# A three-stage kernel on one core: feed-forward groups begun one group later in TensorE's order, a third load buffer, accumulators copied by ScalarE

## The chip, the cores and the metric

The kernel runs on one core of a Trainium2 chip. The metric is device time in microseconds (us) of one execution. Engine names: TensorE (PE in the profile; PEld is its weight load), VectorE (DVE), ScalarE (ACT), GpSimd (POOL) and SyncE (SP), which here issues all the DMAs.

## The reference

Three computations follow each other; sizes are batch 4, sequence 768, model width 384.

```
# 1. a recurrence with a 48x48 state for each of 4 x 8 heads
for t in range(768):
    y[:, :, t] = r_t @ (state + (u * k_t) v_t)
    state = w_t * state + k_t v_t
# 2. a feed-forward block of width 1024 with a convolution over time as its gate
h = max(x @ w_in, 0)                       # 384 -> 1024
x = (h * sigmoid(conv3(h, conv_w))) @ w_out   # 1024 -> 384
# 3. four single-head attention experts (width 64, causal); the two with the larger
#    gate logits are added for each token, with softmax weights
```

## The kernel before, in words

The function `phase1` does steps 1 and 2; the class `Attention` does step 3. A few matmuls of step 3 (the projections of its first batch) run at the end of step 2.

**Recurrence.** It is cut into 32 units: 4 batches x 2 halves of the sequence (384 tokens) x 4 pairs of heads. For unit u there are

- `load(u)`: two DMAs, `wkr` (decays, k and r with the head dimension on the partitions; two buffers) and `rkv` (v, and r and k by token; three buffers);
- `prep(u)`: on VectorE two scans over the decays (L208 `Dp`, L211 `Fp`), then K (L214) and Q (L216); on GpSimd two products (L218, L219), and their sum `e` on VectorE (L221). Dp, K and Q have three buffers, Fp has two;
- `check(u)`: on ScalarE two passes over the decays (L229) that write into Fp's buffer and so come after K;
- `trans(u)`: TensorE transposes K (L252), ScalarE copies it to KT (L254);
- `scores(u)`: TensorE (L238), then GpSimd and VectorE put the masked scores into `AT` (L241, L244);
- `state(u)`: TensorE (L264), VectorE brings the states forward (L268, L271);
- `yout(u)`: TensorE (L285, L291), ScalarE and VectorE split the result into a high and a low part `Y` (L297, L298), and two or four DMAs bring Y into `X` of its half-sequence (L306).

**Feed-forward.** Each of the eight half-sequences, once its X is complete (after four units), has eight groups of 128 hidden columns, 64 groups in all. Group g has `mlp1(g)` (nine matmuls from X, L322, into the only PSUM buffer `hs`; ScalarE reads it out to `ht`, L326), `conv(g)` (ScalarE L335, two steps on VectorE, L341 and L342 in one half and L337 and L339 in the other, Tanh on ScalarE L345, the product `gt` on VectorE L347) and, four groups later (`LAG`), `mlp2(g)` (L360), which adds into three accumulators `x0` to `x2` with one PSUM buffer each. After the eighth group of a half-sequence the accumulators are copied to `xs` and stored; copies 0 and 1 are ScalarE's (L368), copy 2 VectorE's (L366). Inside group 0 to 5 also stand the splits of the feed-forward weights (`split_w`), in groups 8 to 15 a check of them (`check_w`).

**Order.** TensorE's order in this phase is the written one (`tc.manual_schedule`). The order of every other engine's queue, SyncE's among them, is chosen by a planner when the program is built, from its own estimate of times; within a queue instructions run in order. The written loop takes iteration u as: `trans(u)`, group 2u - G0, `scores(u)`, `state(u)`, `load(u+3)`, `check(u-1)`, `yout(u-1)`, `prep(u+1)`, group 2u - G0 + 1, with G0 = 10. A group of this order is `mlp1(g)`, `conv(g)` and `mlp2(g-4)`. The last unit whose Y belongs to a half-sequence has its `yout` in iteration 4, 8, 12 and so on; with G0 = 10 the first group of that half-sequence is the first group of the next iteration.

Of the kernel before, what the change touches and what calls it, by code (L numbers as in the profile page):

```python
# [10 lines left out]
F32 = mybir.dt.float32  # L11
# [14 lines left out]
HP = H // 2  # L26
# [5 lines left out]
NWKR = 1 + NW + 2 * HT  # L32
# [6 lines left out]
LAG = 4  # L39
# [2 lines left out]

LO_ON_DVE = (("win", 3),)
DIAG_ON_DVE = (6, 7, 8)
X2_ON_DVE, V_ON_DVE, OUT_ON_DVE = (2,), (1,), (5,)
SCALED_ON_POOL = 13


# [42 lines left out]
def phase1(tc, nc, a, x2, ident, stat, lim, top, right, left2):  # L91
# [3 lines left out]
    ld = s1.enter_context(tc.tile_pool(name="ld", bufs=3, side="left"))  # L95
# [14 lines left out]
    def split(u):  # L110
        return u // (2 * HP), u // HP % 2, u % HP

    def load(u):
        b, h, hp = split(u)
        q = b * HP + hp
        x = ld.tile([128, NWKR], F32, name="wkr", bufs=2)
        nc.sync.dma_start(x, a["wkr"][q, h])
        z = ld.tile([128, NRKV], F32, name="rkv")
        nc.sync.dma_start(z, a["rkv"][q, h])
        w, k, r = x[:, 0:NW + 1], x[:, NW + 1:NW + 1 + HT], x[:, NW + 1 + HT:]  # L120
        k, r = (y.rearrange("p (c t) -> p c t", c=CH) for y in (k, r))
        v = z[:, 0:2 * CH * 64].rearrange("p (c j e) -> p c j e", c=CH, j=2)
        rn, kn = (z[:, o:o + 2 * CH * D].rearrange("p (j c d) -> p j c d", j=2, c=CH)
                  for o in (2 * CH * 64, 2 * CH * (64 + D)))
        T[u] = dict(w=w, k=k, r=r, rn=rn, kn=kn, v=v)
# [77 lines left out]
    def prep(u):  # L203
        b, h, hp = split(u)
        t = T[u]
        Dp = wk.tile([128, CH, C + 1], F32, name="Dp")
        w = t["w"]
        nc.vector.tensor_tensor_scan(fl(Dp), w[:, 0:NW], fl(cD), 0.0, op0=OP.mult, op1=OP.add)  # L208
        nc.vector.reciprocal(cF[:, :, C:C + 1], Dp[:, :, C:C + 1])
        Fp = wk.tile([128, CH, C + 1], F32, name="Fp", bufs=2)  # L210
        nc.vector.tensor_tensor_scan(fl(Fp)[:, ::-1], w[:, 1:NW + 1][:, ::-1], fl(cF)[:, ::-1], 0.0,  # L211
                                     op0=OP.mult, op1=OP.add)
        K = wk.tile([128, CH, C], F32, name="K")
        nc.vector.tensor_tensor(K, t["k"], Fp[:, :, 1:C + 1], op=OP.mult)  # L214
        Q = wk.tile([128, CH, C], F32, name="Q")
        nc.vector.tensor_tensor(Q, t["r"], Dp[:, :, 0:C], op=OP.mult)  # L216
        m = t["rn"]
        (nc.vector if u in DIAG_ON_DVE else nc.gpsimd).tensor_tensor(m, m, t["kn"], op=OP.mult)  # L218
        nc.gpsimd.tensor_tensor(m, m, u_b[:, hp][:, :, None].to_broadcast([128, 2, CH, D]), op=OP.mult)  # L219
        e = wk.tile([128, 2, CH], F32, name="e")  # L220
        nc.vector.tensor_reduce(e, m, axis=AX.X, op=OP.add)  # L221
        t.update(Dp=Dp, Fp=Fp, K=K, Q=Q, e=e)

    def check(u):
        t = T[u]
        w, Fp = t["w"], t["Fp"]
        wc = w[:, 1:].rearrange("p (c t) -> p c t", c=CH)[:, :, 0:C]
        for z in range(2):
            nc.scalar.activation(Fp[:, :, 0:C], wc, AF.Relu, bias=lim[:, z:z + 1], scale=(-1.0, 1.0)[z],  # L229
                                 accum_out=stat[:, 2 * u + z:2 * u + z + 1])  # L230

    def scores(u):
        t = T[u]
        sc = [ps_s.tile([128, CH, C], F32, name="sc") for j in range(2)]
        for c in range(CH):
            for j in range(2):
                p = slice(64 * j, 64 * j + 64)
                nc.tensor.matmul(sc[j][:, c], t["K"][p, c], t["Q"][p, c], start=True, stop=True)  # L238
        AT = t["AT"] = wk.tile([128, 2, CH, C], F32, name="AT")
        for j in range(2):  # L240
            nc.gpsimd.affine_select(AT[:, j], t["e"][:, j][:, :, None].to_broadcast([128, CH, C]),  # L241
                                    pattern=[[0, CH], [1, C]], compare_op=OP.is_equal, fill=0.0, base=0,
                                    channel_multiplier=-1)
            nc.vector.copy_predicated(AT[:, j], msk, sc[j])  # L244

    def trans(u):
        b, h, hp = split(u)
        t = T[u]
        n = CH - h
        kt = ps_m.tile([128, CH, 128], F32, name="m")  # L250
        for c in range(n):
            nc.tensor.transpose(kt[:, c], t["K"][:, c], ident)  # L252
        KT = t["KT"] = wk.tile([128, CH, 128], F32, name="KT")
        nc.scalar.activation(KT[:, 0:n], kt[:, 0:n], AF.Copy)  # L254

    def state(u):
        b, h, hp = split(u)
        t = T[u]
        n = CH - h
        U = ps_m.tile([128, CH, D], F32, name="m")  # L260
        for c in range(n):
            for j in range(2):
                p = slice(64 * j, 64 * j + 64)
                nc.tensor.matmul(U[p, c], t["KT"][:, c, p], t["v"][:, c, j, 0:D], start=True, stop=True)  # L264
        Sb = Ss[hp]
        P = t["Dp"][:, :, C:C + 1]
        o = CH * h
        nc.vector.tensor_tensor(Sb[:, o:o + n, 0:D], U[:, 0:n], P[:, 0:n].to_broadcast([128, n, D]), op=OP.mult)  # L268
        for c in range(n):
            if o + c:  # L270
                nc.vector.scalar_tensor_tensor(Sb[:, o + c, 0:D], Sb[:, o + c - 1, 0:D], P[:, c], Sb[:, o + c, 0:D],  # L271
                                               op0=OP.mult, op1=OP.add)
# [3 lines left out]
    def yout(u):  # L276
        b, h, hp = split(u)
        t = T[u]
        y = ps_m.tile([128, CH, C], F32, name="m")
        Sb = Ss[hp]  # L280

        for cc in range(CH):
            for j in range(2):
                p = slice(64 * j, 64 * j + 64)
                nc.tensor.matmul(y[p, cc], t["v"][:, cc, j], t["AT"][:, j, cc], start=(cc == 0), stop=False,  # L285
                                 skip_group_check=True)
        for cc in range(CH):
            c = CH * h + cc
            for j in range(2 if c else 0):
                p = slice(64 * j, 64 * j + 64)  # L290
                nc.tensor.matmul(y[p, cc], Sb[p, c - 1], t["Q"][p, cc], start=False, stop=(cc == CH - 1),  # L291
                                 skip_group_check=True)
        Y = wk.tile([128, 2, HT + 4], F32R, name="Y", bufs=2)[:, :, 0:HT + 4 * h]
        if h:
            nc.scalar.activation(Y[:, :, 0:4], _f(YP.pop(hp)), AF.Copy)
        yf = y.rearrange("p c t -> p (c t)")
        nc.scalar.activation(Y[:, 0, 4 * h:], yf, AF.Copy)  # L297
        nc.vector.tensor_tensor(Y[:, 1, 4 * h:], yf, _f(Y[:, 0, 4 * h:]), op=OP.subtract)  # L298
        if not h:
            YP[hp] = wk.tile([128, 2, 4], F32R, name="YP", bufs=HP)  # L300
            nc.scalar.activation(YP[hp], _f(Y[:, :, HT - 4:]), AF.Copy)
        bh = 2 * b + h
        if bh not in X:
            X[bh] = xp.tile([128, 3, 2, HT + 4 * h], F32R, name=f"X{h}")
        for s, n, i, d in _moves(hp):
            nc.sync.dma_start(_f(X[bh][d:d + n, i]), _f(Y[s:s + n]))  # L306
        del T[u]
# [63 lines left out]


    NG = B * 2 * NF
    G0 = 2 * (HP + 1)

    def group(g):
        if 0 <= g < NG:
            mlp1(g)
            conv(g)
        if 0 <= g < 6:  # L380
            split_w(("win", "wout")[g % 2], (win, wout)[g % 2], g // 2 + 1)
        if NF <= g < 2 * NF:
            check_w(("win", "wout")[g % 2], (g - NF) // 2)
        if g == 2 * NF:
            rawc.close()
        if 0 <= g - LAG < NG:
            mlp2(g - LAG)

    with tc.manual_schedule(engines={mybir.EngineType.PE}):
        prep(0)  # L390
        for u in range((NG + LAG + G0 + 1) // 2):
            if u < 2 * NU:
                trans(u)
            group(2 * u - G0)
            if u < 2 * NU:
                scores(u)
                state(u)
                if u + 3 < 2 * NU:
                    load(u + 3)
            if 0 < u <= 2 * NU:  # L400
                check(u - 1)
                yout(u - 1)
            if u + 1 < 2 * NU:
                prep(u + 1)
            if u == 1:
                conv_w()
                split_w("win", win, 0)
            if u == 2:
                split_w("wout", wout, 0)
            if u == 2 * NU:  # L410
                s1.close()
                left2()
            group(2 * u - G0 + 1)

# [631 lines left out]
```

## Time and profile before

| | |
|---|---|
| median of 3 runs | 700.2 us (697.96 to 701.39) |
| the profiled execution's own time | 698.2 us |
| its span, first to last instruction | 696.4 us |
| mean granted TensorE clock | 0.945 of full speed |
| busy: TensorE / its weight loads | 590.6 / 467.8 us |
| busy: VectorE, ScalarE, GpSimd | 510.8, 348.0, 189.3 us |

The profile is one execution, read out by the hardware profiler; its rows are given below, where the prediction needs them. An engine's busy time leaves out its waits; a wait is put down to what ended it. Shares over the whole span mix the two phases, so they are read stage by stage. The granted clock is what the throttle let TensorE have: 1.00 is 2.4 GHz, 0.50 is 1.2 GHz, and a value between them means that a stretch had both.

### The profile page before, as it was taken

The page shows a single profiled execution, that of the slowest core. Times are in us where ns is not written, and L with a number is a line of the kernel's source. Part 1 is how long each engine was busy: PE and PEld are TensorE (multiplying, and loading weights), DVE is VectorE, ACT ScalarE, POOL GpSimd, SP SyncE. Part 2 cuts the span into 40 slices and gives each one's busy share as a digit, 9 for nine tenths or more (in the row PEclk, how much of TensorE's full clock was granted, in tenths as well). Part 3 has the DMA queues.
Part 4 walks back from the last instruction along what each step waited for, and adds up shares of the span by engine and source line. Part 5 has one row for each costly group of instructions (what it writes and reads, how often), then busy time and mean ns, then how long its engine had stood idle before and what let it go on. Part 6 is the DMA issues. An engine that isn't in the chain of part 4 may idle for free. (4 is left out here: it accounts for less than half of the span.)

```text
span 696.4 us, 11267 instructions
## 1 busy us (share of the span) xinstructions
PE 590.6 (85%) x3978; PEld 467.8 (67%) x3978; DVE 510.8 (73%) x1163; ACT 348.0 (50%) x843; POOL 189.3 (27%) x209
## 2 busy tenths in 40 slices
PE   3352588897997997989989999998999899899996
PEld 3231466675765775666767677696898788789664
DVE  7999569788786987787986565378875777587471
ACT  3252684444454453544443445265555655556462
POOL 7677123223142321332231062002002100300360
PEclk9975679899999999999989999999999999999999
DMA  8487674444352553443431255236415432551502
GB/s 308 157 306 226 229 245 118 121 143 130 105 170 80 153 149 94 151 141 99 148 92 46 69 167 164 61 102 171 102 54 152 128 91 66 147 137 59 147 2 72
DMA packets 34400, 92.38 MB, mean 133 GB/s; under 512 B 5024, under 2 KB 14368, under 8 KB 34336
## 3 DMA queue, kind: packets, MB, share of 16 engines
q1 hardware_dynamic: 34336, 91.59, 44.6%
q8 instruction: 33, 0.54, 0.3%
q14 instruction: 31, 0.25, 0.1%
HBM read 53.77 MB, written 9.44 MB: 91 GB/s over the span
## 5 line engine op out<-in xcount | busy, mean ns | idle before, releaser
L322 PE MATMUL hs<-X,win 128*128 128x384 f32 (+1 forms) x576 | 127.4, 368 | 46.4 <-DMA X<-Y 15.1
L322 PEld LDWEIGHTS hs<-X,win 128*128 128x128 f32 x576 | 105.0, 200 | 56.7 <-issue 16.3
L360 PE MATMUL x<-gt,wout 128*128 128x386 f32 (+1 forms) x384 | 140.0, 502 | 2.4 <-DVE xs L366 2.4
L360 PEld LDWEIGHTS x<-gt,wout 128*128 128x128 f32 x384 | 75.1, 198 | 41.7 <-DVE xs L366 5.3
L782 ACT ACTIVATE A<-sm,mn 128x128 f32<-128x128 f32 (+5 forms) x96 | 63.7, 665 | 26.3 <-DVE mn L781 25.7
L229 ACT ACTIVATE Fp<-wkr,lim 128x384 f32<-128x384 f32 x64 | 39.1, 611 | 69.1 <-DVE K L214 61.9
L218 POOL TENSOR_TENSOR rkv<-rkv 128x288 f32<-128x288 f32 x29 | 30.6, 1054 | 147.8 <-DMA rkv<-in_rkv 141.8
L781 DVE CUSTOM_DVE_ANT_0 sm<-st,mask 128x128 f32<-128x128 f32 (+5 forms) x96 | 58.0, 618 | 16.6 <-PE st L768 16.1
L345 ACT ACTIVATE st<-ct 128x382 f32<-128x382 f32 (+1 forms) x64 | 33.4, 521 | 54.6 <-DVE ct L342 29.2
L241 POOL TENSOR_SCALAR_AFFINE_SELECT AT<-e 128x384 f32<-128x384 f32 x64 | 44.6, 719 | 49.9 <-DVE e L221 49.9
L347 DVE SCALAR_TENSOR_TENSOR gt<-st,ht 128x382 f32<-128x382 f32 (+1 forms) x64 | 37.5, 587 | 24.0 <-ACT st L345 22.8
L802 PE MATMUL t<-ident,A 128*128 128x128 f32 x336 | 53.5, 275 | 1.7 <-ACT T L806 0.9
L768 PE MATMUL st<-sk,sq 128*128 128x384 f32 (+3 forms) x128 | 44.4, 358 | 3.1 <-DVE mn L781 2.2
L680 POOL TENSOR_TENSOR xs<-x,xs 128x768 fp32r<-128x768 f32 x12 | 22.4, 1882 | 87.5 <-ACT xs L679 87.5
L244 DVE COPY_PREDICATED AT<-msk,sc 128x384 f32<-128x384 uint32 x64 | 36.1, 585 | 13.5 <-PE sc L238 13.5
L808 DVE COPY T<-t 128x128 f32<-128x128 f32 (+3 forms) x64 | 32.2, 504 | 18.6 <-PE t L802 18.1
L802 PEld LDWEIGHTS t<-ident,A 128*128 128x128 f32 x336 | 40.4, 140 | 7.5 <-POOL A L795 1.9
L768 PE MATMUL st<-sl,sq 128*128 128x384 f32 (+3 forms) x128 | 40.9, 333 | 4.9 <-DMA sl<-kl 4.8
L326 ACT ACTIVATE ht<-hs 128x384 f32<-128x384 f32 (+1 forms) x64 | 30.8, 482 | 27.1 <-PE hs L322 26.9
L818 PE MATMUL m<-T,V 128*64 128x384 f32 (+2 forms) x288 | 43.3, 421 | 0.0
L219 POOL TENSOR_TENSOR rkv<-rkv,u_b 128x288 f32<-128x288 f32 x32 | 35.2, 1100 | 29.5 <-DVE rkv L218 25.0
L341 DVE SCALAR_TENSOR_TENSOR ct<-ht,cwk,ct 128x386 f32<-128x386 f32 x32 | 25.1, 785 | 23.0 <-ACT ct L335 23.0
(129 smaller groups left out, 1167.9 us busy)
## 6 DMA issues: line engine op xcount, KB each, us to landing
wkr<-in_wkr SPq DMA_DIRECT2D x32, 578.0 KB, 4.6
rkv<-in_rkv SPq DMA_DIRECT2D x32, 480.0 KB, 3.5
rawt<-in_win SPq DMA_DIRECT2D x8, 768.0 KB, 5.1
rawt<-in_wout SPq DMA_DIRECT2D x8, 768.0 KB, 5.1
sk<-kh SPq DMA_DIRECT2D x32, 192.0 KB, 3.3
sl<-kl SPq DMA_DIRECT2D x32, 192.0 KB, 4.1
x<-x SPq DMA_DIRECT2D x12, 384.0 KB, 4.2
out_dram<-ot SPq DMA_DIRECT2D x24, 192.0 KB, 2.0
```

The lines of the kernel that those rows point to most:

```text
L219: nc.gpsimd.tensor_tensor(m, m, u_b[:, hp][:, :, None].to_broadcast([128, 2, CH, D]), op=OP.mult)
L229: nc.scalar.activation(Fp[:, :, 0:C], wc, AF.Relu, bias=lim[:, z:z + 1], scale=(-1.0, 1.0)[z], accum_out=stat[:, 2 * u + z:2 * u + z + 1])
L241: nc.gpsimd.affine_select(AT[:, j], t["e"][:, j][:, :, None].to_broadcast([128, CH, C]), pattern=[[0, CH], [1, C]], compare_op=OP.is_equal ...
L244: nc.vector.copy_predicated(AT[:, j], msk, sc[j])
L322: nc.tensor.matmul(hs[:, 0:N], win[wi][:, f // 2, i, (f % 2) * 128:(f % 2 + 1) * 128], x[:, i, xi], start=(n == 0), stop=(n == 8))
L347: nc.vector.scalar_tensor_tensor(gt, st, 1.0, ht[:, o:o + N], op0=OP.add, op1=OP.mult)
L360: nc.tensor.matmul(acc[0][i][:, 0:N], wout[:, f, i * 128:(i + 1) * 128], gt, start=(f == 0), stop=(f == NF - 1))
L768: nc.tensor.matmul(st[:, z, 0:n], q[:, qi * C:(qi + 1) * C], k[:, z * n:(z + 1) * n], start=(i == 0), stop=(i == 1))
L781: nc.vector.tensor_tensor_reduce(o3, i3, m3, 1.0, 3e38, op0=OP.add, op1=OP.min, accum_out=mn)
L782: nc.scalar.activation(at, o3, AF.Exp, bias=mn, scale=-1.0, accum_out=rs[:, qi % 3:qi % 3 + 1])
L802: nc.tensor.transpose(pt[:, ki - k0], at[:, ki * C:(ki + 1) * C], self.ident)
L818: nc.tensor.matmul(po[o, lo:HT], V[:, ki, (2 * p + j) * 64:(2 * p + j + 1) * 64], Ts[j][:, ki, lo:], start=(ki == 0), stop=(ki == n - 1))
```

## The change

Three edits. `G0` becomes 11, so that group 2u - 11 follows `trans(u)` and group 2u - 10 ends the iteration: every group stands one place later in TensorE's order against the recurrence, and the first group of a half-sequence is no longer next to the last of the one before; the loop gets one turn more to hold the last group. `wkr` takes the pool's own three buffers in place of two. The third accumulator's copy goes from VectorE to ScalarE.

```diff
-X2_ON_DVE, V_ON_DVE, OUT_ON_DVE = (2,), (1,), (5,)
+X2_ON_DVE, V_ON_DVE, OUT_ON_DVE = (), (1,), (5,)
...
     def load(u):
-        x = ld.tile([128, NWKR], F32, name="wkr", bufs=2)
+        x = ld.tile([128, NWKR], F32, name="wkr")
...
-    G0 = 2 * (HP + 1)
+    G0 = 2 * (HP + 1) + 1
...
-        for u in range((NG + LAG + G0 + 1) // 2):
+        for u in range((NG + LAG + G0 + 2) // 2):
```

## Rows read from the trace of the kernel before

**Rows 1.** Windows by stage: length, busy PE, PEld, DVE, ACT, POOL, PEclk, DMA, GB/s.

```profile
0.00:70.76 70.76, 24.98 (x213) 18.82 (x213) 65.19 (x97) 25.65 (x59) 51.39 (x58) 0.80 0.76 250
70.76:124.63 53.87, 38.82 (x287) 31.33 (x287) 39.47 (x76) 35.32 (x78) 12.24 (x16) 0.82 0.61 198
124.63:360.93 236.30, 214.64 (x1527) 161.22 (x1527) 191.95 (x361) 108.94 (x267) 69.45 (x80) 0.96 0.43 127
360.93:404.35 43.42, 42.24 (x283) 31.55 (x283) 24.79 (x52) 18.31 (x43) 6.49 (x14) 0.93 0.23 66
404.35:452.24 47.89, 45.67 (x200) 34.60 (x199) 25.03 (x33) 22.41 (x46) 14.71 (x14) 1.00 0.46 128
452.24:696.40 244.16, 224.29 (x1474) 190.29 (x1474) 164.38 (x547) 137.41 (x352) 35.07 (x30) 0.99 0.38 102
```

**Rows 2.** TensorE's timeline, first group and one border: start, us, instructions, idle before.

```profile
70.76 3.25 PE L322 MATMUL hs<-X,win 128*128 128x384 f32 x9 [10.81 <-DMA X<-Y]
...
163.35 1.88 PE L322 MATMUL hs<-X,win 128*128 128x388 f32 x9
...
167.01 0.38 PE L252 MATMUL m<-ident,K 128*128 128x128 f32 x2
...
171.44 2.29 PE L322 MATMUL hs<-X,win 128*128 128x384 f32 x9 [4.05 <-DMA X<-Y]
173.52 3.31 PE L360 MATMUL x<-gt,wout 128*128 128x386 f32 x6
...
179.47 1.83 PE L322 MATMUL hs<-X,win 128*128 128x384 f32 x9
...
183.09 0.38 PE L252 MATMUL m<-ident,K 128*128 128x128 f32 x2
```

**Rows 3.** Six gaps before a half-sequence's first group, by windows: one, and their sum.

```profile
118.71:124.63 5.92, 0.49 (x5) 0.28 (x3) 5.65 (x10) 1.53 (x5) 1.43 (x2) 0.72 0.49 141
...
sum 26.68, PE 2.25 PEld 1.21 DVE 25.40 ACT 9.03 POOL 8.54; mean PE 0.37 PEld 0.20 DVE 4.23 ACT 1.50 POOL 1.42
```

**Rows 4.** The first group behind each of these gaps: one, and the sum of six.

```profile
360.93:367.76 6.83, 6.83 (x17) 4.60 (x17) 4.11 (x9) 3.71 (x10) 1.31 (x2) 0.55 0.11 23
...
sum 34.20, PE 34.00 PEld 23.99 DVE 14.91 ACT 15.95 POOL 6.15; mean PE 5.67 PEld 4.00 DVE 2.48 ACT 2.66 POOL 1.02
```

**Rows 5.** VectorE's waits, 124.63 to 360.93: engine, line, ender, total us, times, longest.

```profile
DVE gt L347 <- ACT st L345: 14.6, 20, 1.3
DVE ct L341 <- ACT ct L335: 12.1, 12, 3.4
DVE ct L337 <- ACT ct L335: 5.8, 8, 1.5
DVE AT L244 <- PE sc L238: 5.5, 5, 1.5
DVE e L221 <- POOL rkv L219: 2.3, 2, 1.6
```

**Rows 6.** VectorE's timeline: a subtraction for Y, two scans, a wait between them.

```profile
167.28 0.54 DVE L298 TENSOR_TENSOR Y<-m,Y 128x384 fp32r<-128x384 f32 x1
...
203.41 0.96 DVE L208 TENSOR_TENSOR_SCAN Dp<-wkr,cD 128x387 f32<-128x387 f32 x1
...
210.25 0.62 DVE L337 SCALAR_TENSOR_TENSOR ct<-ht,cwk,ct 128x381 f32<-128x381 f32 x1 [0.47 <-ACT ct L335]
...
214.35 1.56 DVE L208 TENSOR_TENSOR_SCAN Dp<-wkr,cD 128x387 f32<-128x387 f32 x1
```

**Rows 7.** SyncE's queue at the same border.

```profile
167.85 2.55 SPq L306 DMA_DIRECT2D X<-Y  x4
```

**Rows 8.** ScalarE's timeline: accumulator copies, and a check behind K.

```profile
192.53 0.86 ACT L368 ACTIVATE xs<-x 128x386 f32<-128x386 f32 x2
...
206.95 0.61 ACT L229 ACTIVATE Fp<-wkr,lim 128x384 f32<-128x384 f32 x1 [2.92 <-DVE K L214]
```

**Rows 9.** Groups by line: VectorE's accumulator copies, whole span.

```profile
L366 DVE COPY xs<-x 128x382 f32<-128x382 f32 (+1 forms) x8 | 4.4, 549 | 6.1 <-PE x L360 6.1
```

## The prediction, made before the change was run

> **What bounds the kernel now.** I read the busy shares by stage first, because the kernel is two programs in a row: a first phase with the recurrence and the feed-forward groups, and attention after it. [rows 1] cut the span at the starts of TensorE's feed-forward groups. The reader is to see three things. In the prologue (0 to 70.76 us) VectorE is busy 65.19 us and TensorE 24.98, so VectorE sets the pace. In the long middle, 124.63 to 360.93, TensorE is busy 214.64 of 236.30 us and VectorE 191.95: neither is full. From 452.24 on TensorE is busy 224.29 of 244.16 us, and the diff touches nothing there.
>
> Second, TensorE's timeline at one border between two half-sequences [rows 2]. The last group before the border ends, two transposes follow at 167.01, and the next group's first matmul starts at 171.44 after 4.05 us of idleness that the DMA into X ended. The half-sequence is eight groups, and such a gap comes back with each, every 236.30 / 5 = 47.3 us; [rows 3] hold six of them, 26.68 us in all, in which TensorE worked 2.25 us.
>
> Third, what the other engines did in these gaps: in the same [rows 3] VectorE was busy 25.40 of the 26.68 us. So TensorE waits for X, but X is late because VectorE is behind. In [rows 6] the subtraction that makes the low part of X runs at 167.28, almost 4 us after the matmuls that it reads (they ended as the group at 163.35 began [rows 2]); [rows 7] show SyncE issuing the four pieces from 167.85 for 2.55 us, and then they fly.
>
> Last, the price behind a gap: the first group after the one shown runs from 171.44 to the end of the output matmuls at 176.83 [rows 2], 5.39 us. The same two lines later, at full clock, go from 179.47 to 183.09, 3.62 us. [rows 4] show the worst of the six, 6.83 us at a mean granted clock of 0.55, that is for the most part at 1.2 instead of 2.4 GHz; before each of them TensorE had stood still, as [rows 3] show.
>
> **The change part by part.**
>
> *Groups one slot later.* Before, an iteration was: transposes, even group, scores and state and output of the recurrence, odd group. The even group that opens a half-sequence came right behind the last group of the one before. After, the opener moves to the end of its iteration. Between the output matmuls whose result X needs and X's first use there were one group and the transposes (163.35 to 167.39); now there are a group (3.66), transposes (0.38), a group (3.62) and the scores to outputs (from 176.83 to 179.47, 2.64): 10.3 us. X arrived 8.1 us after 163.35. So the wait for X goes, with 2 us to spare. All that a group issues moves along, its ScalarE and VectorE instructions too; the weight splits and checks traced inside a group were not held to their place before (the queues of the other engines are the planner's), so I move them by nothing.
>
> How much of this reaches the end? TensorE's side of the middle: its five gaps (the sum less the one shown [rows 3]) are 20.76 us with 1.76 us of work in them, 19.0 lost; the five slow first groups behind the borders that lie at or after its start (the sum less the one shown [rows 4]) are 34.20 - 6.83 = 27.37 us against 5 x 3.62 = 18.1, 9.3 lost. Together 28. VectorE's side is less, and VectorE is what was busy in the gaps. Its idle time there by cause is in [rows 5]. The waits for the scores matmuls, 5.5 us, are there because TensorE stood still. The waits for ScalarE's first convolution product are 12.1 + 5.8 = 17.9 us in 20 waits; away from a border one is 0.47 [rows 6], so at least 17.9 - 20 x 0.47 = 8.5 of it is the border's. The wait for rkv, 2.3, follows from a load whose buffer TensorE freed late. That makes 16.3 us that VectorE can win back. The waits for tanh (14.6 us, 20 of them) are the ping-pong of two in-order queues in every iteration and stay. That they are VectorE's own period shows in [rows 6]: the scan recurs at 203.41 and 214.35, 10.94 us apart, with no border between, while TensorE needs the 10.3 summed above. I take VectorE's 16.3, not TensorE's 28, since its row is the nearer one (95% busy in the gaps); 28 stays as the end of the range.
>
> *All accumulators by ScalarE.* Eight VectorE copies of 549 ns go [rows 9], five of them in the middle: 2.7 us off the pacing engine. ScalarE copies two in 0.86 us [rows 8], so a third costs it 0.43, on an engine busy 108.94 of 236.30 us [rows 1]. Behind the copies the next half-sequence's first output matmuls wait, since the accumulators have one buffer. Three in a row end 0.43 us after two, 3.4 us over eight borders if TensorE waited for each; before, the third was VectorE's at 549 ns. I cost it at nothing, under the cover of the matmuls of the group in between; if the copies are caught behind a wait of ScalarE, see the third rival.
>
> So the rows make the third copy no slower on ScalarE than on VectorE [rows 8, 9]. The Trainium skill, "TensorEngine Tiling (Array Packing)", section "PSUM Bottleneck", says to use both ScalarE and VectorE for emptying PSUM; this part of the change does the opposite. By that rule the gain would be the 3.4 us smaller; by the rows it is not, because VectorE is the engine with the queue, and no run so far shows all three on one engine.
>
> *Third load buffer.* No row of [rows 5] is a wait for wkr, so in the middle it buys nothing. In the prologue it lets the third unit's load leave earlier, and VectorE may then take the recurrence before the weight splits. VectorE's idle time there is 70.76 - 65.19 = 5.6 us [rows 1]; TensorE's wait for the first X is 10.81 us [rows 2]. A gain is between 0 and 10.81, a loss up to about 5.6 if the larger first burst delays what VectorE needs. I take 0: VectorE is 92% busy and reordering makes no less work.
>
> *First stage, 70.76 to 124.63.* Now scores, state and outputs (2.6 us at full clock) fit into the 10.81 us wait for the first X, and the gap at 118.71 (5.92 us with 0.49 of work [rows 3], so 5.4) goes. The ends are 0 and 8. VectorE is idle 53.87 - 39.47 = 14.4 us of this stage [rows 1], a larger share than in the middle, so more of it can be won than there. I take 5.
>
> *Last stage, 360.93 to 404.35.* VectorE is busy 24.79 of 43.42, so TensorE paces. The slow first group, 6.83 against 3.62 us, is won back: 3.
>
> *End of the first phase.* One more group now comes after the recurrence. TensorE is 45.67 of 47.89 us busy there, so its 3.6 us count, less some 1.8 us of VectorE work that leaves the paced part (two convolution steps of 0.6 and a product of 0.56, an estimate from the same stretch): -2.
>
> **Sum.** 16.3 + 2.7 + 5 + 3 - 2 = 25 us off the profiled execution's 698.2 (span 696.4 and 1.8 around it): 673. That execution lies 0.3% below the median of 700.2, inside the runs' spread of 697.96 to 701.39, so I make nothing of the difference.
>
> **The rivals.**
>
> *TensorE paces.* If the planner's new queues cost VectorE fewer waits than today's, the gain is TensorE's: 28 in the middle, 8 and 3 in the stages around it, less 2: 37, time 661. For it: VectorE's 191.95 us of work would fit. Against it: a scan period above TensorE's 10.3.
>
> *The wait changes its name.* VectorE is already behind in the gaps; what it now does in them has to be done elsewhere. If every gap only spreads into short waits of TensorE for K's transposed copy, what remains is the slow clock (9.3 + 3) less 2: about 10, time 688. For it: 25.40 of 26.68. Against it: VectorE's 16.3 us of border idleness is counted in rows.
>
> *Slower: the three copies queue behind ScalarE's wait for K.* ScalarE's queue is in order; at 206.95 it had waited 2.92 us for VectorE's K, to run two checks of 0.61 us [rows 8]. If the planner puts the copies behind that, TensorE's output matmuls wait 2.92 + 1.2 + 1.3 = 5.4 us at seven borders, 38 us: 25 won, 38 lost, time 711. It decides from 25 / 7 = 3.6 us per border on. Against it: today's two copies at 192.53 [rows 8] are placed ahead of such a wait. The Trainium skill's "PSUM Bottleneck" in "TensorEngine Tiling (Array Packing)", use both engines, points this way; no row here shows such a price.
>
> *The move does nothing*, since the planner shifts the recurrence by as much: 698 to 701. Against it: TensorE's order is written by hand.
>
> **How the numbers follow.** VectorE paces (my forecast): 0.60, with 659 to 687 for its own range (below, the prologue's 10.81 and the first stage's 8; above, the first stage's 0, the copies' 3.4 and the prologue's 5.6). TensorE paces: 0.13. The wait changes its name: 0.15, three quarters of it faster by over 0.5%, the rest within. Slower: 0.07. Nothing: 0.05. About 0.5% is what a measurement of this kernel tells from no change. Faster 0.60 + 0.13 + 0.11 = 0.84, same 0.09, slower 0.07. From 656 to 692 the range holds the first two and half of the third.
>
> **What would show it.** Right: no wait of a group's first matmul for X at the borders; a first group at full clock in about 3.6 us; eight groups in 43 to 44 us instead of 47; scans 10.8 to 11.3 us apart throughout; short waits of TensorE once an iteration for the transposed K or the scores' operands. Wrong: borders with gaps of 3 us or more of any name; the accumulators' copies behind a ScalarE wait; a first group that starts much before or after 70 us; or attention that is longer than 244 us, since its order is the planner's and I cost it at 0 with TensorE's 19.9 idle us there as the most that could move.

## The result: 700.8 to 677.0 us, and the profile after the change

The changed kernel took 676.98 us (median of 4 runs, 671.73 to 680.83), the kernel before, beside it on the same chip, 700.8 us (697.96 to 701.82). The ratio is 0.9661, 95% interval 0.959 to 0.9733. The forecast was 673 us with a range of 656 to 692, faster at 0.84. The total came out as forecast; its terms did not, and the experiments are about them.

The stages of the profiled execution after (676.99 us, span 675.2), cut as [rows 1]; only the last cut differs, it is the end of the last output matmul, which lies at 451.77 in the trace before:

```profile
0.00:71.69 71.69, 32.66 (x256) 24.82 (x257) 65.40 (x99) 26.98 (x63) 47.74 (x56) 0.66 0.71 243
71.69:114.06 42.37, 36.63 (x286) 29.02 (x287) 38.77 (x73) 32.04 (x73) 16.49 (x18) 0.93 0.81 273
114.06:340.98 226.92, 209.74 (x1527) 158.10 (x1527) 197.63 (x368) 111.47 (x281) 68.19 (x80) 0.98 0.44 131
340.98:378.40 37.42, 36.24 (x241) 27.49 (x239) 20.76 (x42) 16.55 (x36) 6.32 (x13) 1.00 0.30 88
378.40:426.08 47.68, 45.69 (x200) 34.59 (x198) 24.24 (x31) 22.57 (x46) 13.34 (x11) 1.00 0.42 117
426.08:675.20 249.12, 228.75 (x1475) 192.84 (x1474) 164.71 (x546) 139.07 (x354) 35.30 (x31) 0.97 0.38 100
```

Against [rows 1] the prologue lost 0.9 us, the first stage won 11.5, the five middle half-sequences 9.4, the seventh 6.0, the rest of the first phase lost 0.3 and attention 4.5: 21.2 us of span.

TensorE at a border after, and one of the two slow groups that are left in the middle; the first answers to [rows 2]:

```profile
158.38 0.87 PE L291 MATMUL m<-Q,Ss 64*64 64x128 f32 x12
159.18 1.84 PE L322 MATMUL hs<-X,win 128*128 128x384 f32 x9
160.85 2.11 PE L360 MATMUL x<-gt,wout 128*128 128x386 f32 x6
...
131.01 2.57 PE L322 MATMUL hs<-X,win 128*128 128x388 f32 x9 [2.22 <-ACT ht L326]
133.38 3.05 PE L360 MATMUL x<-gt,wout 128*128 128x382 f32 x6
```

The half-sequence's first group at 159.18 follows the outputs without a gap and takes 3.8 us. The wait for X is gone at every border of the middle. What TensorE waits for instead, in 114.06 to 340.98 (all its waits there but those under 0.2 us), and the longest wait of ScalarE in the same stretch:

```profile
PE hs L322 <- ACT ht L326: 10.5, 11, 2.2
PE m L264 <- ACT KT L254: 6.7, 6, 1.5
```

```profile
ACT Fp L229 <- DVE K L214: 54.9, 19, 5.0
```

10.5 + 6.7 = 17.2 is the whole of TensorE's idle time there (226.92 - 209.74). Both are readouts that ScalarE does late. TensorE's and ScalarE's timelines show one such wait:

```profile
183.88 0.49 PE L252 MATMUL m<-ident,K 128*128 128x128 f32 x3
...
190.13 0.56 PE L264 MATMUL m<-rkv,KT 128*64 128x48 f32 x12 [1.39 <-ACT KT L254]
```

```profile
183.29 0.61 ACT L335 ACTIVATE ct<-ht,cwk 128x382 f32<-128x382 f32 x1
188.25 0.62 ACT L229 ACTIVATE Fp<-wkr,lim 128x384 f32<-128x384 f32 x1 [4.34 <-DVE K L214]
...
189.60 0.47 ACT L254 ACTIVATE KT<-m 128x384 f32<-128x384 f32 x1
190.20 0.52 ACT L345 ACTIVATE st<-ct 128x382 f32<-128x382 f32 x1
190.63 0.47 ACT L326 ACTIVATE ht<-hs 128x384 f32<-128x384 f32 x1
```

The transposes had ended by 184.4. ScalarE stood idle from 183.9 to 188.25, because the next instruction of its queue was a decay check of a later unit, which writes over Fp and so waits for that unit's K. KT, ready to be copied for four microseconds, stood behind it, and ht behind KT.

### The profile page after: what moved, and what is told of

It is laid out like the page before. It is cut to its first block, busy times and chain, and to the rows that moved or that the text cites. A ratio compares the mean times of both kernels' runs of the same rounds, so it can differ in the third digit from the quotient of the medians.

```text
span 675.2 us, 11262 instructions
## 1 busy us (share of the span) xinstructions
PE 589.7 (87%) x3978; PEld 466.9 (69%) x3978; DVE 511.5 (76%) x1155; ACT 348.7 (52%) x851; POOL 187.4 (28%) x209
## 4 chain that ended last, share of the span: by engine, by line
PE 41%; DVE 31%; ACT 11%; DMA 9%; issue 5%; SPq 1%; POOL 1%; DVEq 0%; ACTq 0%; POOLq 0%
PE m L694 7%; PE x L360 6%; PE st L768 5%; PE m L818 5%; PE hs L322 4%; PE t L802 4%; DVE Dp L208 4%; PE m L830 3%; DVE Ss L271 3%; PE m L724 3%; DVE Fp L211 3%; ACT st L345 2%; ACT Fp L229 2%; DMA X<-Y 2%; DVE AT L244 2%
## 5 line engine op out<-in xcount | busy, mean ns | idle before, releaser
L322 PE MATMUL hs<-X,win 128*128 128x384 f32 (+1 forms) x576 | 122.7, 359 | 17.5 <-ACT ht L326 15.4
L360 PE MATMUL x<-gt,wout 128*128 128x386 f32 (+1 forms) x384 | 135.0, 489 | 0.0
L322 PEld LDWEIGHTS hs<-X,win 128*128 128x128 f32 x576 | 101.7, 194 | 28.2 <-ACT ht L326 20.4
L360 PEld LDWEIGHTS x<-gt,wout 128*128 128x128 f32 x384 | 72.9, 192 | 35.8 <-issue 1.2
L768 PE MATMUL st<-sk,sq 128*128 128x384 f32 (+3 forms) x128 | 46.0, 370 | 3.6 <-DVE mn L781 2.7
L238 PEld LDWEIGHTS sc<-Q,K 64*128 64x128 f32 x384 | 28.1, 212 | 23.0 <-issue 15.2
L806 ACT ACTIVATE T<-t 128x512 f32<-128x512 f32 (+3 forms) x64 | 28.5, 446 | 26.8 <-PE t L802 22.0
L238 PE MATMUL sc<-Q,K 64*128 64x128 f32 x384 | 35.2, 318 | 7.1 <-DVE AT L244 7.1
L335 ACT ACTIVATE ct<-ht,cwk 128x382 f32<-128x382 f32 (+1 forms) x64 | 39.3, 614 | 1.7
```

The source lines that it names most:

```text
L322: nc.tensor.matmul(hs[:, 0:N], win[wi][:, f // 2, i, (f % 2) * 128:(f % 2 + 1) * 128], x[:, i, xi], start=(n == 0), stop=(n == 8))
L360: nc.tensor.matmul(acc[0][i][:, 0:N], wout[:, f, i * 128:(i + 1) * 128], gt, start=(f == 0), stop=(f == NF - 1))
L768: nc.tensor.matmul(st[:, z, 0:n], q[:, qi * C:(qi + 1) * C], k[:, z * n:(z + 1) * n], start=(i == 0), stop=(i == 1))
```

## The experiments

Twelve kernels were run. This table holds their medians (us), their ratios to the kernel before on the same chip with 95% intervals, and their stages (us, one profiled execution each; cuts as above).

| kernel | median | ratio | prologue | first | middle five | seventh | rest | attention |
|---|---|---|---|---|---|---|---|---|
| before | 700.8 | 1 | 70.76 | 53.87 | 236.30 | 43.42 | 47.42 | 244.63 |
| after | 676.98 | 0.9661 (0.959 to 0.9733) | 71.69 | 42.37 | 226.92 | 37.42 | 47.68 | 249.12 |
| e1 move alone | 684.41 | 0.9782 (0.9748 to 0.9816) | 71.25 | 50.71 | 225.77 | 37.42 | 47.60 | 250.15 |
| e2 buffer alone | 690.1 | 0.9861 (0.9804 to 0.9918) | 69.29 | 44.66 | 236.29 | 41.15 | 47.45 | 248.36 |
| e3 copies alone | 699.75 | 1.001 (0.9977 to 1.0043) | 70.15 | 54.09 | 236.36 | 43.54 | 47.22 | 244.74 |
| e4 G0 = 12 | 676.02 | 0.9684 (0.9654 to 0.9714) | 70.49 | 47.14 | 223.36 | 39.39 | 45.38 | 248.14 |
| e5 after, copy on VectorE | 674.46 | 0.9646 (0.9598 to 0.9695) | 70.08 | 44.18 | 225.81 | 37.43 | 47.62 | 248.08 |
| e6 after, one convolution step | 671.52 | 0.9625 (0.9579 to 0.9671) | 69.80 | 44.12 | 224.79 | 37.44 | 45.19 | 248.16 |
| e7 after, no decay checks | 670.45 | 0.9589 (0.9541 to 0.9637) | 66.31 | 51.69 | 221.64 | 37.43 | 47.39 | 247.34 |
| e8 before, no weight checks | 690.3 | 0.9876 (0.9832 to 0.9921) | 68.10 | 45.32 | 238.50 | 43.55 | 47.83 | 246.70 |
| e9 after, checks in own buffer | 686.71 | 0.9849 (0.9798 to 0.9899) | 66.20 | 50.70 | 236.04 | 37.43 | 47.38 | 244.15 |
| e10 spread order | 657.47 | 0.9415 (0.937 to 0.946) | 70.78 | 44.48 | 207.85 | 37.52 | 47.28 | 247.39 |
| e11 e9 and e10 | 689.7 | 0.9869 (0.9817 to 0.9921) | 68.31 | 49.33 | 235.75 | 37.50 | 47.46 | 248.85 |
| e12 spread, G0 = 11 | 676.29 | 0.9694 (0.9656 to 0.9732) | 71.16 | 42.94 | 222.32 | 41.00 | 46.76 | 246.82 |

### e1 to e3: each edit alone

e1 is the kernel before with

```diff
-    G0 = 2 * (HP + 1)
+    G0 = 2 * (HP + 1) + 1
-        for u in range((NG + LAG + G0 + 1) // 2):
+        for u in range((NG + LAG + G0 + 2) // 2):
```

> The kernel before with G0 = 11 and the longer loop alone; two wkr buffers and VectorE's third copy stay. Theory (the move carries the result; the copies give VectorE's 549 ns per half-sequence, the buffer nothing): 677 + 3 to 4, so 680 to 682, and no wait for X at the borders. Rival, the buffer is needed (with two, a load waits for the check of the unit two ahead and a scan waits for its wkr): 688 or more, with VectorE waits for wkr. Rival, the copies are needed (the copy stands in VectorE's queue and the next half-sequence's output matmuls wait for it): 685 or more, with waits of L360 for VectorE's xs at each border.

684.41 us, above the theory's 680 to 682 and below the rivals' 685 and 688: no wait for X was left at a border, as the theory said, but none of the three had the time. The stages say why: the move won the middle (10.5 us) and the seventh half-sequence (6.0), and only 3.2 of the 11.5 us of the first stage.

e2 is the kernel before with

```diff
-        x = ld.tile([128, NWKR], F32, name="wkr", bufs=2)
+        x = ld.tile([128, NWKR], F32, name="wkr")
```

> The kernel before with three wkr buffers alone. Theory: no gain in the middle, since no wait there is for wkr; the prologue moves by less than 2 us; 698 to 702. Rival, VectorE gets ahead with earlier loads and X comes sooner at the borders: 690 to 695, with border gaps under 3 us.

690.1 us: the time is the rival's, the place is neither's. The middle is unmoved (236.29), the first stage is 9.2 us shorter.

e3 is the kernel before with

```diff
-X2_ON_DVE, V_ON_DVE, OUT_ON_DVE = (2,), (1,), (5,)
+X2_ON_DVE, V_ON_DVE, OUT_ON_DVE = (), (1,), (5,)
```

> The kernel before with all three accumulators copied by ScalarE alone. Theory: VectorE is what makes X late at the borders, so its 0.55 us per border come off the gaps: 8 x 0.55 = 4.4 us at most, 696 to 699. Rival, three copies in a row hold the next output matmuls 0.43 us longer at each border: 700 to 704.

No stage differs by more than 0.6 us. The ratios of the three, taken off 1, are 2.2, 1.4 and -0.1%, together 3.5 of the 3.4% that the change won: the move and the buffer add up, the copies are nothing.

### e5: the copies, with the rest in place

```diff
-X2_ON_DVE, V_ON_DVE, OUT_ON_DVE = (), (1,), (5,)
+X2_ON_DVE, V_ON_DVE, OUT_ON_DVE = (2,), (1,), (5,)
```

> The changed kernel with the third accumulator's copy given back to VectorE. Theory (alone the copies moved the time by nothing; with the move in place VectorE paces, so its 0.55 us per half-sequence count): 677 + 2.7 to 4.4, so 679 to 682. Rival (queue order decides and the copies cost nothing wherever they stand): 676 to 678.

674.46 us, ratio 0.9646 against the changed kernel's 0.9661, in its interval. The theory falls, and the time lies a little below even the rival's 676 to 678: eight copies of 549 ns [rows 9] given back to VectorE cost nothing that the runs show.

### e8: where the buffer's 9 us came from

```diff
-        if NF <= g < 2 * NF:
-            check_w(("win", "wout")[g % 2], (g - NF) // 2)
```

> The kernel before without the checks of the feed-forward weights (eight loads of 768 KB and sixteen passes of ScalarE of 0.9 to 1.0 us are left out); two wkr buffers stay. It asks where the third buffer's 9 us in the first stage come from. Theory (in the kernel before, ht of the second group stands in ScalarE's queue behind some five weight checks, 9.08 us of TensorE's time at 89.15; the third buffer only makes the planner order that queue otherwise): the first stage goes from 53.87 to 45 to 47, the whole to 690 to 692. Rival (the recurrence itself comes late for lack of a wkr buffer): the first stage stays at 51 or more, the whole at 697 or more.

First stage 45.32, total 690.3, as the theory said. The queue itself can be read. In the kernel before, ScalarE around the second group's ht, and TensorE's next group:

```profile
82.15 0.90 ACT L186 ACTIVATE rawt<-rawt 128x768 f32<-128x768 f32 x1 [0.20 <-DMA rawt<-in_wout]
...
85.70 0.88 ACT L186 ACTIVATE rawt<-rawt 128x768 f32<-128x768 f32 x1 [1.15 <-DMA rawt<-in_win]
...
87.08 0.96 ACT L187 ACTIVATE rawt<-rawt,lim 128x768 f32<-128x768 f32 x1
...
88.63 0.47 ACT L326 ACTIVATE ht<-hs 128x384 f32<-128x384 f32 x1
```

```profile
78.02 1.83 PE L322 MATMUL hs<-X,win 128*128 128x384 f32 x9
79.69 0.38 PE L252 MATMUL m<-ident,K 128*128 128x128 f32 x2
89.15 3.25 PE L322 MATMUL hs<-X,win 128*128 128x384 f32 x9 [9.08 <-ACT ht L326]
```

The group's matmuls end at 79.85, and five passes of weight checks, two decay checks and a wait for the check's own load run on ScalarE before ht. With the third buffer alone (e2) the same pair of groups on TensorE:

```profile
75.38 1.83 PE L322 MATMUL hs<-X,win 128*128 128x384 f32 x9
...
79.95 3.25 PE L322 MATMUL hs<-X,win 128*128 128x384 f32 x9 [2.32 <-ACT ht L326]
```

Here the weight checks are still run, but the planner's queue has them between the readouts, not in front of one. So what the buffer bought is another order of ScalarE's queue. That it acts by the planner's estimate, and not by a load that in fact arrives sooner, is argued from these rows; no run held the order fixed. Three buffers alone do not keep the gain: e7 and e9 (below) have them, and their first stages are 51.69 and 50.70 us long. In e7 ht stands behind the conversion of a feed-forward weight, which waits for GpSimd, and TensorE's next group waits 6.44 us for it:

```profile
74.35 0.84 ACT L175 ACTIVATE win<-wm 128x768 fp32r<-128x768 f32 x1 [7.21 <-POOL wm L80]
```

### e4: one more place later

```diff
-    G0 = 2 * (HP + 1) + 1
+    G0 = 2 * (HP + 1) + 2
```

> The changed kernel with G0 = 12, so that every group stands one more place later: the first group of a half-sequence is again next to the last group of the one before, but a whole iteration after the recurrence's outputs. Theory (what counts is that X has some 8 us from the output matmuls to its first use; more slack buys nothing, and one more group comes behind the recurrence): 677 + 2 to 4, so 679 to 681, no wait for X. Rival, more slack lets VectorE's lead grow and the short waits go: 668 to 674. Rival, it is the parity that counts (two groups of different half-sequences side by side): back to 685 or more.

676.02 us. Two writings that put the opening group next to, or not next to, the one before end in one time, so the parity is not what counts; nor does more room help the whole (the middle is 3.6 us shorter, the first stage 4.8 longer).

In the middle of e4 TensorE's output matmuls wait 4.6 us, in four waits, for ScalarE's accumulator copies. One copy, of three that follow each other in the changed kernel, is caught behind a decay check that waits for K, and the output matmuls at 189.89 wait 2.23 us for it:

```profile
188.75 0.62 ACT L229 ACTIVATE Fp<-wkr,lim 128x384 f32<-128x384 f32 x1 [3.60 <-DVE K L214]
...
189.37 0.47 ACT L368 ACTIVATE xs<-x 128x386 f32<-128x386 f32 x1
```

That is the prediction's slower rival, come true in a small way; in the changed kernel no output matmul waits for a copy.

### e6: does VectorE pace?

e6 takes L339 and L342 out of the changed kernel:

```diff
-            nc.vector.scalar_tensor_tensor(ct, ht[:, 1:N + 1], w[:, 2, f:f + 1], ct, op0=OP.mult, op1=OP.add)
...
-            nc.vector.scalar_tensor_tensor(ct[:, 0:N - 1], ht[:, 3:N + 2], w[:, 2, f:f + 1], ct[:, 0:N - 1],
-                                           op0=OP.mult, op1=OP.add)
```

> The changed kernel without the second convolution step (the term that reads one token ahead is left out), which takes 0.6 us x 64 off VectorE and nothing off TensorE or ScalarE. Theory (VectorE paces the middle at some 11.3 us per iteration, 1.2 of it this step): the five middle half-sequences go from 226.9 to 208 or TensorE's 4 x 10.3 x 5 = 206, and the whole to 650 to 660. Rival (TensorE, with its waits for ht and KT that come from ScalarE's queue, paces): the middle stays above 220 and the whole above 668.

The whole is just inside the rival's bounds, the middle moved by 2.1 us. Its window, TensorE's first waits, and ScalarE's:

```profile
113.92:338.71 224.79, 207.96 (x1526) 158.02 (x1526) 168.85 (x322) 112.34 (x281) 66.51 (x80) 0.98 0.45 132
```

```profile
PE m L264 <- ACT KT L254: 14.1, 17, 1.9
PE hs L322 <- ACT ht L326: 2.7, 2, 2.1
```

```profile
ACT Fp L229 <- DVE K L214: 46.4, 20, 5.1
```

VectorE lost 28.8 of its 197.63 us of work and stands idle for 55.9, yet TensorE waits for almost as long as before (16.8 us), and ScalarE still stands 46.4 us behind K. My theory, that VectorE's work paces the middle, falls here. Of VectorE's idle time 51.0 us are waits for ScalarE's products and tanh, while ScalarE waits for K; that this loop is what makes K late is argued from the waits. The edit also gave ScalarE another queue: KT now stands behind a tanh in 9 of 20 units, and the waits for KT grew from 6.7 to 14.1 us. What less work on VectorE would win with ScalarE's queue held as it was is not shown.

### e7 and e9: the check in ScalarE's queue

e7 drops `check(u - 1)` from the loop and zeroes its flags.

> The changed kernel without the decay checks (both passes of ScalarE over the decays of each unit are left out). ScalarE no longer waits for VectorE's K in its queue and does 1.2 us less in each iteration. Theory (VectorE's work paces; ScalarE's wait for K is a consequence): the middle falls by less than 5 us, mostly by shorter waits of VectorE for ScalarE's tanh; 670 to 676. Rival (the two in-order queues wait for each other, and ScalarE's 54.9 us behind K in the middle are a link of it): the middle falls by 10 us or more, 660 to 667.

TensorE's waits for KT are gone from the middle and those for ht are not (12.1 us):

```profile
PE hs L323 <- ACT ht L327: 12.1, 12, 2.0
PE m L253 <- DVE Ss L269: 0.7, 2, 0.5
```

The middle won 5.3 us, nearer to the theory's 5 than to the rival's 10, though "VectorE's work paces" had no part in it (e6). The whole says less of this than the middle does, since the prologue became 5.4 us shorter and the first stage 9.3 longer. e9 keeps the checks and takes their dependence away:

```diff
-            nc.scalar.activation(Fp[:, :, 0:C], wc, AF.Relu, bias=lim[:, z:z + 1], scale=(-1.0, 1.0)[z],
+            ck = wk.tile([128, CH, C], F32, name="ck", bufs=1)
+            nc.scalar.activation(ck, wc, AF.Relu, bias=lim[:, z:z + 1], scale=(-1.0, 1.0)[z],
```

> The changed kernel with the decay checks writing into a buffer of ScalarE's own instead of over Fp, so that they need only the loaded decays and no longer come after VectorE's K; the work is the same. Theory formed after the run without the second convolution step (TensorE sets the period, and what it loses goes by ScalarE's in-order queue: KT stands behind a check that waits for K): ScalarE's 54.9 us behind K go, TensorE's waits for KT (6.7 us in the middle) go with them, those for ht (10.5) stay, since without the checks they stood behind tanh waiting for the convolution; middle 226.9 to 218 to 222, whole 668 to 672. Rival (the checks' 1.2 us of work an iteration is what was won when they were left out, not the wait): middle 225 or more, whole 675 to 678.

A miss on both sides: 686.71 us, and the middle is back at 236.04. TensorE's waits, and ScalarE's longest:

```profile
PE hs L323 <- ACT ht L327: 15.8, 9, 2.2
PE m L265 <- ACT KT L255: 12.1, 9, 2.6
```

```profile
ACT ck L230 <- DMA wkr<-in_wkr: 65.3, 18, 6.1
```

```profile
195.13 0.61 ACT L230 ACTIVATE ck<-wkr,lim 128x384 f32<-128x384 f32 x1 [6.12 <-DMA wkr<-in_wkr]
...
195.74 0.47 ACT L255 ACTIVATE KT<-m 128x384 f32<-128x384 f32 x1
```

Free of K, the check was put still further ahead, where it waits for its load, and KT and ht stand behind it as they did. That is the mechanism again with another ender: what TensorE loses here (27.9 us) is waits for readouts, and they are late by what stands ahead of them in ScalarE's queue.

### e10 to e12: another order of TensorE's work

e10 changes TensorE's written order instead of the queue: scores stand between the iteration's two groups, state and outputs behind the second.

```diff
             group(2 * u - G0)
             if u < 2 * NU:
                 scores(u)
-                state(u)
                 if u + 3 < 2 * NU:
                     load(u + 3)
+            group(2 * u - G0 + 1)
+            if u < 2 * NU:
+                state(u)
...
-            group(2 * u - G0 + 1)
```

with G0 = 12.

> The changed kernel with TensorE's order spread: transposes, group 2u - 12, scores, group 2u - 11, state, outputs; so each group's ht has 3 us or more until the next group's first matmul instead of 2.5 on one side, KT has two groups instead of one, and X has more than an iteration. Theory (TensorE's period is its work plus waits for ScalarE's queue): the waits for KT go and those for ht shrink, 10 to 17 us in the middle, 1 to 2 us lost behind the recurrence; whole 662 to 668. Rival (K's lateness on VectorE only moves: then TensorE waits for scores' K, for KT or for X for the same time under another name): whole 674 to 680.

657.47 us, ratio 0.9415: better than both kernels, and 5 us below the theory's range. The middle's window, and TensorE's only wait there:

```profile
115.26:323.11 207.85, 206.43 (x1528) 153.75 (x1527) 188.84 (x363) 118.07 (x281) 66.49 (x80) 1.00 0.49 140
```

```profile
PE m L252 <- DVE Ss L268: 3.3, 5, 1.8
```

TensorE is busy 206.43 of 207.85 us at full clock (a wait can lie under the modelled end of a matmul), with the same matmuls as in the changed kernel (x1528 against x1527). ScalarE's wait for K fell to 16.7 us and no readout is late. Against the changed kernel the middle is 19.1 us shorter, of which G0 = 12 alone gives 3.6 (e4).

The edit meant to give the readouts more time, and the way from the transposes to the first use of KT did grow, from 5.5 to 8.0 us on average. But the readouts also came earlier. In the changed kernel KT's copy began 3.99 us after its transposes on average (at most 5.29), in e10 0.09 us (at most 0.18); ht's began 2.36 us after its matmuls (at most 4.92), now 0.30 (at most 1.68). One unit's rows, a check and KT of ScalarE's timeline and between them the transposes of TensorE's:

```profile
160.94 0.62 ACT L229 ACTIVATE Fp<-wkr,lim 128x384 f32<-128x384 f32 x1 [1.59 <-DVE K L214]
...
166.52 0.44 PE L252 MATMUL m<-ident,K 128*128 128x128 f32 x2
...
167.13 0.38 ACT L254 ACTIVATE KT<-m 128x256 f32<-128x256 f32 x1
```

In the changed kernel the instruction just ahead of KT is a check in 19 of 20 units; here it is a readout of the recurrence's output in all 20 (L297 or L295). So with TensorE's new order the planner wrote another queue for ScalarE too. An estimate from these figures: 8.0 us would have covered KT even at its old lateness, but the 2.7 us that the closest pair of groups leaves for ht would not have covered ht's. How the 19.1 us divide between the new order and the new queue is not shown; no run held one of them fixed.

e11 is e9's and e10's edits together.

> Both: the spread order of TensorE and the checks in ScalarE's own buffer. Theory (both take away the same waits for KT, and each some of its own): 658 to 666, not more than 4 us below the better of the two. Rival (VectorE becomes the bound at some 11 us an iteration): no better than the spread order alone, within 1.5 us of it, with VectorE busy 95% or more in the middle.

689.7 us, again a miss on both sides. The check waits for its load (51.2 us in the middle), and now TensorE's transposes wait for VectorE's Ss (24.1 us). The early check is what e9 and e11 share; how it makes VectorE's Ss late here is not shown.

e12 is e10 with G0 = 11.

> The spread order with G0 = 11 instead of 12: the first group of a half-sequence stands as the second group of the iteration behind its last outputs, some 5 us after them (transposes 0.4, a group 3.7, scores 0.9), not 10. It asks how much room X needs. Theory (the way from the output matmuls to X is two splits of 0.5 us, 2.6 us of issuing four pieces and some 4.3 us of flight, 7.5 to 8 us without any lateness of VectorE): a wait for X of 2.5 to 3 us comes back at seven borders, with the slow clock behind it, so 657 + 20 to 35, less 2 for one group fewer behind the recurrence: 675 to 690. Rival (X was late at the borders because VectorE was late, and with VectorE on time 5 us is enough): no wait for X, 654 to 657.

676.29 us, in the theory's 675 to 690, by less than it said: the waits for X came back at the first five of the seven borders, 1.6 to 2.5 us before the group and at the first border 0.5 us more inside it, 10.6 us in all. The profile puts two of them down to another ender, among them the row at 204.92; there, too, the group starts 0.1 us after X's first piece has landed (204.83).

```profile
158.54 3.16 PE L322 MATMUL hs<-X,win 128*128 128x384 f32 x9 [2.52 <-DMA X<-Y]
204.92 2.46 PE L322 MATMUL hs<-X,win 128*128 128x388 f32 x9 [1.95 <-ACT st L345]
249.91 2.94 PE L322 MATMUL hs<-X,win 128*128 128x384 f32 x9 [2.30 <-DMA X<-Y]
```

From the end of the outputs to the group's start it was 6.5 to 7.3 us at the four of these borders where VectorE began its part of Y 1.3 to 2.0 us behind the outputs (3.9 us in the kernel before, [rows 2, 6]), and 8.1 at the first, where VectorE was 5.3 us behind. So 5 us of room is too little even with VectorE nearly on time, and about 7 us is what X needs then.

## Why the prediction was right, and where it was not

**The wait for X goes, with 2 us to spare.** Right that it goes: no gap at a border (e1 and after). The 2 us to spare were less sure than they looked. X needs about 7 us when VectorE is nearly on time (e12), but in the changed kernel VectorE began its part of Y 2.3 to 5.7 us behind the outputs at the borders of the middle. At 293.53 X's last piece had landed 0.6 us before the group began, and TensorE had waited 1.26 us for KT in between. The room of 10.3 us plus such waits was enough.

**The middle, 16.3 + 2.7 = 19.** Over-estimated: 9.4 (10.5 by the move alone). The step that failed is the choice of VectorE's account over TensorE's. VectorE's idle time came out nearly as sized: it fell from 44.4 to 29.3 us, 15.1 against 16.3. But that was not the time won, because VectorE's busy time rose by 5.7 us although the copies left; 5.2 of it is in the 40 steps that bring the states forward (before, then after; busy us and mean ns behind the bar), for a reason that the rows do not show:

```profile
L271 DVE SCALAR_TENSOR_TENSOR Ss<-Ss,Dp 128x48 f32<-128x48 f32 x40 | 12.3, 307 | 1.0
L271 DVE SCALAR_TENSOR_TENSOR Ss<-Ss,Dp 128x48 f32<-128x48 f32 x40 | 17.5, 438 | 0.9
```

By TensorE's account, the middle before had 236.30 - 214.64 = 21.7 us of idleness [rows 1] and the slow groups [rows 4]. After, idleness is 17.2, 4.5 less, and busy time 214.64 - 209.74 = 4.9 less with the same count of matmuls, which is clock. The border's waits went, and ht and KT took their place: for the idle part the rival "The wait changes its name" was nearly right, and for the clock half of the 9.3 us came, since two waits of 2.0 and 2.2 us for ht still had slow groups behind them. e6 shows that VectorE's work was not the bound, e10 that the waits for ScalarE's readouts were: "TensorE paces", the rival at 0.13, is reached once no readout is late (28.5 us in the middle against its 28). The sign that the prediction gave for its own account, eight groups in 43 to 44 us, did not come: they took 226.92 / 5 = 45.4.

**The copies.** Cost 0 for ScalarE was right in the changed kernel; in e4 it was 4.6 us of TensorE's waits. The 2.7 us that they were to win on VectorE were 0 (e3, e5), for the same reason as above. The Trainium skill, "TensorEngine Tiling (Array Packing)", section "PSUM Bottleneck", says to use both ScalarE and VectorE for emptying PSUM. Against that, e3's 1.001 (0.9977 to 1.0043) and e5 show neither a loss nor a gain from one engine emptying all three accumulators; e4's waits point the way of the page, but no run shows e4 with the third copy on VectorE.

**The third buffer, 0.** Wrong: 9.2 us alone (e2). I looked for a wait named wkr and found none, which was true and beside the point. In the first stage the wait to ask about was the 9.08 us for ht at 89.15: what stands ahead of ht in ScalarE's queue, and who put it there.

**First stage, 5.** Under-sized: 11.5, of which the move alone gave 3.2.

**Last stage, 3, and one more group behind the recurrence, -2.** Measured 6.0 and -0.3. The slow first group was won back as said (6.00 us of span, 42.24 to 36.24 busy at clock 0.93 and 1.00), but the stage also holds 42 matmuls fewer, x283 to x241, and the prologue 43 more. With the groups one place later the recurrence runs one unit further ahead, in the prologue, where TensorE waits anyway; that pays for the group at the end.

**Attention, 0.** It took 4.5 us more. TensorE's busy time rose by 4.5 (224.29 [rows 1] to 228.75) with the same count of matmuls (x1474 and x1475), so this is clock and not a wait. The prediction had named an attention longer than 244 us as a sign of being wrong; whether the change or the single execution brought it is open.

The sum of 25 thus held two large errors of opposite sign, the middle (-9.6) and the first stage (+6.5), beside +4.7 for the end of the phase, -4.5 for attention and -0.9 for the prologue: 21.2. That they nearly cancel is luck: the right total is no proof of the step that it was built on. Of the rivals, "the copies queue behind ScalarE's wait for K" named the right queue and the right wait, but in the changed kernel the wrong victim: KT and ht, not the copies (in e4 the copies too).

## What to carry to other kernels

When an in-order engine reads out TensorE's results, look at what stands ahead of each readout in its queue, and ask what that instruction waits for; relieving the engine that is late won 2.1 us of the middle in e6, while another order of TensorE's own work, with which the readouts came on time, won 19.1 in e10. The Trainium skill, "Perfetto Trace Analysis", section "Optimization Strategies", advises to optimize the engines that block the critical path; in e6, where VectorE was the late one, taking work off it won little. Removing a dependence from a side task can make things worse where a planner orders the queue: in e9 the task was then put further ahead. And where a planner orders queues, a buffer count, or another order of one engine, can be an edit of every queue: read the stage where queues hold the most optional work, not only the waits that carry the buffer's name.

## What the hardware showed that I had not expected

Short stand-stills of TensorE can be followed by the lower clock, but their length alone does not decide it. In the attention of the trace before, TensorE stood still for 1.34 us and then ran at a granted clock of 1.00 (2.4 GHz):

```profile
604.74 0.62 PE L694 MATMUL m<-xs,wq 128*128 128x384 f32 x2 [1.34 <-ACT xs L679]
...
604.74:614.74 10.00, 8.94 (x53) 8.38 (x54) 9.05 (x31) 7.36 (x21) 1.83 (x1) 1.00 0.31 79
```

At the same place after the change it stood still for 1.77 us, and the next 10 us ran at 0.66, for the most part at 1.2 GHz; so did the group behind the 2.22 us at 131.01:

```profile
580.94 0.61 PE L694 MATMUL m<-xs,wq 128*128 128x384 f32 x2 [1.77 <-ACT xs L679]
...
580.94:590.94 10.00, 8.94 (x36) 8.25 (x37) 6.63 (x22) 5.58 (x17) 1.83 (x1) 0.66 0.31 80
...
131.01:136.43 5.42, 5.42 (x17) 3.84 (x17) 4.11 (x9) 3.95 (x10) 1.30 (x2) 0.69 0.41 140
```

Behind the 1.39 us at 190.13 the clock stayed at 1.00. It also stayed there in e5 behind the same wait of 2.22 us at the same group, whose nine matmuls then took 1.87 us in place of 2.57:

```profile
131.22 1.87 PE L322 MATMUL hs<-X,win 128*128 128x388 f32 x9 [2.22 <-ACT ht L326]
```

What else decides is not shown. Over the runs attention's length follows the clock for the most part: 244.15 us with 223.60 busy at a mean of 1.00 (e9), 244.63 with 224.29, 247.39 with 227.38 (e10), 249.12 with 228.75; what is left is 20.0 to 20.7 us in twelve of the fourteen kernels, 21.2 in e1 and 22.1 in e6. Whether the slow slices belong to a kernel or to an execution is open: each kernel was profiled once.
